# Soft-MoE behind a sliding-window attention: how two experts' w2 come in, as whole transfers or as 112 partitions and twice 8

## The chip, the cores and the metric

One core of one Trainium2 chip runs the whole program. The metric is the time of one execution on the device in microseconds, lower is better. "TensorE" is the matmul engine (PE), "VectorE" DVE, "ScalarE" ACT, "GpSimd" POOL, "SyncE" SP. Sixteen DMA engines move data between HBM and the core's on-chip memory of 128 partitions.

## The reference, cut to what matters

```python
# attention: q, k, v of [8, 8, 576, 64]; band of 32 for four heads, every fourth of 128 for the others
scores = np.where(mask, (q @ k.T) / 8, -1e9); attn = softmax(scores); x = (attn @ v) -> [4608, 512]

logits = x @ phi                                   # [4608, 32]: 8 experts of 4 slots
d = softmax over the 4608 rows of logits;  slot_input = d.T @ x
for e in range(8):
    slot_out[e] = np.maximum(slot_input[e] @ w1[e], 0) @ w2[e]   # w1 [512, 1024], w2 [1024, 512]
out = softmax over the 32 slots of logits @ slot_out             # [4608, 512], float32
```

All eight experts' output rows are needed before the first row of `out` can be made, so every w2 is needed first.

## The kernel before, in words

The order of the work is written out by hand (`manual_schedule`): each engine runs its instructions in the order of the program text. The eight batches go through attention in a pipeline (`ORDER`, `STEPS`). The inputs are float32 in HBM and are cast to half precision by the transfers on their way in, so all loads are issued by POOL, which is one queue, in order.

The loads, in POOL's order: for each batch two transfers each of raw Q, K and V (`load_raw`, L191, 64 partitions each); between them, from batch 3 on, one w1 of 1 MB (half precision) at a time (`load_w1`, L197); behind the last V the remaining w1 and the w2 of experts 0, 1 and 2 (`load_w2` without `s`, L205: one transfer of 128 partitions, 8 KB in each). Then a place in on-chip memory has to come free: the raw tiles and the slabs of Q and K are given back once the last transposes and scores of batch 7 have run (the test on `left`, L555). There w2 of experts 3 and 4 come as one whole transfer each (L205 again), and w2 of experts 5, 6 and 7 as twelve quarters of 256 KB (L211): the left 256 columns of 5, 6, 7 (two quarters each), then the right 256 columns.

Each load of POOL counts its landing on one of eight semaphores, in turn. An issue waits until the transfer eight issues before it, which used the same semaphore, has landed. So at most eight transfers are in flight, and where the queue is full POOL stands and waits for a landing before it issues the next.

After attention, PE multiplies the slots by all w1 (L616), transposes (L626), and sums w2 into two column halves `so0` and `so1` (`emit_so`, L646): experts 0 to 3 for both halves, expert 4 for both halves, then 5, 6, 7 for the left half, each as its quarters land. The left half is gathered and spread (L660, L665), and the first six batches of `out` are made for the left 256 columns (L672 on PE, L681 on ACT, L685 on DVE, sent by L692); the right half's experts 5, 6, 7 are worked in between, and `spread_so(1)` opens the rest of the output: six right halves, two whole batches, and the two transfers of left-over rows (L721). Output transfers are issued by POOL too, on the same queue behind the loads.

Of the kernel before, what the change touches and what calls it, by code (L numbers as in the profile page):

```python
# [10 lines left out]
FP16 = mybir.dt.float16  # L11
# [13 lines left out]
DMODEL = H * D  # L25
E_EXP = 8
S_PER_E = 4
N_SLOTS = 32
# [10 lines left out]
NP = 5  # L39
NFIN = N_ROWS // 128  # L40
DH = DMODEL // 2

GROUPS = (
    (("P", 0), ("P", 1), ("P", 2)),
# [3 lines left out]
ORDER = """  # L48
MD0.2 MK2.2 AP4.2 ET.3 VBc.1 S1.1 MK0.1 RP4.2 ED.3 E1.1 AD1.2 EP.3 VC.1 RD1.2 MP4.2
VCc.1 ER.3 MD1.2 AD3.2 VA.1 QT0.0 AP3.2 RD3.2 VAc.1 QT1.0 RP3.2 MD3.2 S2.1 KT1.0  # L50
# [45 lines left out]
def kernel(  # L96
# [10 lines left out]
    nc = tc.nc  # L107
# [5 lines left out]
    consts = ctx.enter_context(tc.tile_pool(name="consts", bufs=1))  # L113
# [9 lines left out]
    phi_raw = consts.tile([128, 4, N_SLOTS], FP16, name="phi_raw")  # L123
    phi4 = consts.tile([128, 4, 4, N_SLOTS], FP16, name="phi4")
    ones = consts.tile([128, 128], FP16, name="ones")
    ET = consts.tile([128, 192 * B], FP16, name="ET")
    UT = consts.tile([128, 5, N_SLOTS], FP32, name="UT")
    rcol = consts.tile([128, N_SLOTS], FP32, name="rcol")
# [9 lines left out]
    w2t = {e: w2a_pool.tile([128, 8, DMODEL], FP16, name=f"w2_{e}", tag=f"w2_{e}") for e in range(3)}  # L138
# [13 lines left out]
    def slab_weights(e, tag, n):  # L152
        t = fix.tile([128, n], FP16, name=f"w2_{e}", tag=tag)
        w2t[e] = t[:, 0 : 8 * DMODEL].rearrange("p (c n) -> p c n", c=8)
# [41 lines left out]
    def load_w1(e):  # L196
        nc.gpsimd.dma_start(  # L197
            out=w1t[e].rearrange("p (u c) f -> p u (c f)", u=2),
            in_=moe_w1[e].rearrange("(u p c) f -> p u (c f)", u=2, p=128),
        )  # L200

    def load_w2(e, s=None):
        src = moe_w2[e].rearrange("(p c) n -> p c n", p=128)
        if s is None:
            nc.gpsimd.dma_start(  # L205
                out=w2t[e].rearrange("p c n -> p (c n)"), in_=src.rearrange("p c n -> p (c n)")
            )
            return
        cols = slice(DH * s, DH * s + DH)
        for u in range(2):  # L210
            nc.gpsimd.dma_start(out=w2t[e][:, 4 * u : 4 * u + 4, cols], in_=src[:, 4 * u : 4 * u + 4, cols])  # L211
# [195 lines left out]
    def back_et(b, lp):  # L407
        nc.scalar.activation(out=ET[:, 192 * b : 192 * b + 192], in_=lp, func=AF.Exp, scale=1.0)

    def back_erow(b):  # L410
        m, l = et_cols(b)
        ep = ring.tile([128, 6, N_SLOTS], FP16, name=f"ep_{b}", tag="ring")
        left = ET[0:32, l : l + 128]
        nc.tensor.transpose(
            ep[:, 0:4, :].rearrange("p t s -> p (t s)"), ET[:, m : m + 128], ident
        )
# [14 lines left out]
    def back_erd(b):  # L431
        m = et_cols(b)[0]
        erd = s_pool.tile([128, DIL, N_SLOTS], FP16, name=f"erd_{b}", tag="erd")
        nc.vector.transpose(out=erd, in_=ET[:, m : m + 128].rearrange("p (a r) -> p r a", r=DIL))
        erd_t[b] = erd
# [38 lines left out]
    for which in "QK":  # L474
        load_raw(which, 1)
    nc.gpsimd.dma_start(
        out=phi_raw.rearrange("p (u c) s -> p u (c s)", u=2),
        in_=moe_phi.rearrange("(u p c) s -> p u (c s)", u=2, c=2),
# [4 lines left out]
    nc.vector.memset(ones, 1.0)  # L483
    nc.vector.memset(ET, 0.0)
    nc.vector.memset(siTm, 0.0)
# [10 lines left out]
    def step(op, b):  # L496
        if op[0] in "ARM" and op[1:] in TILES:
            kind, i = TILES[op[1:]]
            if op[0] == "A":
                tmp[(op[1:], b)] = emit_av(b, kind, i)  # L500
            elif op[0] == "R":
                tmp[("R" + op[1:], b)] = emit_recip(b, kind, i, tmp[(op[1:], b)])
            else:
                engine = nc.scalar if op[1:] in ON_ACT else nc.vector
                norm_mult(b, kind, i, tmp.pop((op[1:], b)), tmp.pop(("R" + op[1:], b)), engine)
        elif op in ("S0", "S1", "S2"):
            tmp[(op, b)] = emit_scores(b, int(op[1]))
        elif op in ("E0", "E1", "E2"):
            emit_exp(b, int(op[1]), tmp.pop(("S" + op[1], b)))
        elif op in ("MK0", "MK1", "MK2"):  # L510
            emit_mask(b, int(op[2]))
        elif op[0:2] in ("QT", "KT", "VT"):
            turn(op[0], b, int(op[2]))
        elif op in ("XP0", "XP1"):
            tmp[(op, b)] = xT_plain(b, int(op[2]))
        elif op in ("XD0", "XD1"):
            tmp[(op, b)] = xT_dil(b, int(op[2]))
        elif op in ("XPc0", "XPc1", "XDc0", "XDc1"):
            xT_copy(b, op[1], int(op[3]), tmp.pop((op[0:2] + op[3], b)))
        elif op in ("VA", "VB", "VC", "VD"):  # L520
            tmp[(op, b)] = v_rows(b, "ABCD".index(op[1]))
        elif op in ("VAc", "VBc", "VCc", "VDc"):
            v_place(b, "ABCD".index(op[1]), tmp.pop((op[0:2], b)))
        elif op in ("LG", "EP"):
            tmp[(op, b)] = (back_logits if op == "LG" else back_erow)(b)
        elif op == "ET":
            back_et(b, tmp.pop(("LG", b)))
        elif op == "ER":
            back_er(b, tmp.pop(("EP", b)))
        else:  # L530
            {"ED": back_erd, "U": back_u, "UT": back_add}[op](b)

    def loads(which, b):
        load_raw(which, b)
        if which == "V":
            if b > 2:
                load_weights(1)
            if b == B - 1:
                load_weights(len(weights))
# [5 lines left out]
    w2b_pool = None  # L545
    for it in range(B + max(s for _, s in STEPS)):
        for op, stage in STEPS:
            b = it - stage
            if not 0 <= b < B:
                continue  # L550
            step(op, b)
            if op in frees and b + 2 < B:
                loads(frees[op], b + 2)
            left.discard((op, b))
            if w2b_pool is None and not left:  # L555
                raw_pool.release()
                w2b_pool = tc.alloc_tile_pool(name="w2b", bufs=1, side="right")
                for e in (3, 4, 5):
                    w2t[e] = w2b_pool.tile([128, 8, DMODEL], FP16, name=f"w2_{e}", tag=f"w2_{e}")
                slab_weights(6, "qk0", QK_SLAB)  # L560
                slab_weights(7, "qk1", QK_SLAB)
                for e in (3, 4):
                    load_w2(e)
                for s in range(2):
                    for e in (5, 6, 7):
                        load_w2(e, s)
        if it == 0:
            nc.vector.tensor_copy(
                out=phi4, in_=phi_raw[:, :, None, :].broadcast_to([128, 4, 4, N_SLOTS])
            )  # L570
# [17 lines left out]
    for pr in range(B // 2):  # L588
# [11 lines left out]
        out=diag,  # L600
# [10 lines left out]
    for fc in range(2):  # L611
        for g in range(2):
            for dc in range(4):
                for j in range(4):
                    e = 4 * g + j
# [9 lines left out]
    for c in range(8):  # L625
# [3 lines left out]
        out=hTm[:, 0].rearrange("p c (j s) -> p c j s", j=4)[:, :, :, 0:16], in_=hT4[:, :, :, 0:16]  # L629
    )  # L630
    nc.scalar.copy(
        out=hTm[:, 1].rearrange("p c (j s) -> p c j s", j=4)[:, :, :, 16:32], in_=hT4[:, :, :, 16:32]
# [5 lines left out]
    om_l = h_pool.tile([128, B // 2, DMODEL], FP16, name="om_l", tag="om_l")  # L638
    so = [psum_so.tile([128, DH], FP32, name=f"so{s}", tag=f"so{s}") for s in range(2)]

    def emit_so(s, experts):
        for c in range(8):
            for e in experts:
# [4 lines left out]
                    hTm[:, g, c, 32 * j : 32 * j + 32],  # L648
                    w2t[e][:, c, DH * s : DH * s + DH],
                    start=(e < 4 and c == 0),  # L650
# [3 lines left out]
    def part_cols(s):  # L654
        c0 = DH * s
        return (nc.vector.tensor_copy, 0, c0), (nc.scalar.copy, DH // 2, c0 + DH // 2)

    def gather_so(s):
        for copy, c, c0 in part_cols(s):
            copy(out=so_part[:, c0 : c0 + DH // 2], in_=so[s][:, c : c + DH // 2])  # L660

# [58 lines left out]
    for e in range(2):  # L720
        nc.gpsimd.dma_start(  # L721
            out=rest[:, e, 512:576, :].rearrange("n i d -> i n d"), in_=om_l[64 * e : 64 * e + 64]
# [37 lines left out]
```

## Time and profile before

| what | value |
|---|---|
| median of 3 runs | 181.05 us (180.69 to 181.62) |
| the profiled execution | 180.9 us, its span 178.9 us |
| granted TensorE clock, mean | 0.853 |
| busy share of PE, DVE, ACT, POOL | 72%, 70%, 68%, 31% |
| chain that ended last: DMA, DVE, PE, ACT | 52%, 16%, 11%, 9% |
| of it, transfers of the weights | 36% |
| HBM read and written | 62.07 MB and 9.44 MB, 400 GB/s over the span |

The span is the profiled stretch; 2.0 us of the execution lie around it. The profile's DMA row gives, for 40 equal slices of 4.47 us, the mean busy share of the sixteen DMA engines in tenths, and the GB/s row what they moved, counted on the receiving side: a load receives half as many bytes as it reads from HBM, since it casts float32 to half precision, and an output transfer twice as many as it reads. A line of the DMA issues says how many transfers, how large on the receiving side, and how many microseconds from the issue to the last landing. A waiting time is put down to what ended it.

### The profile page before, as it was taken

The numbers are of one execution on the slowest core, as the hardware profiler recorded it, in microseconds if no ns is written. First come the engines' busy times: TensorE is split into PE (matmuls) and PEld (weight loads), VectorE is DVE, ScalarE is ACT, GpSimd is POOL, SyncE is SP. The second block draws the span as 40 slices with busy tenths as digits, with TensorE's granted clock in tenths as the row PEclk, the third lists the DMA queues.
The fourth block names the chain that finished last, engine by engine and source line by source line (L and its number), as shares of the span: only waits on it lengthen the run. The fifth ranks groups of instructions, "written<-read, shape, count | busy, mean of one in ns | idle before, by whom it ended". The sixth has DMA issues, their size and how long they took to land.

```text
span 178.9 us, 5405 instructions
## 1 busy us (share of the span) xinstructions
PE 128.0 (72%) x2316; PEld 84.7 (47%) x2316; DVE 125.7 (70%) x274; ACT 122.2 (68%) x267; POOL 56.2 (31%) x94
## 2 busy tenths in 40 slices
PE   0026838989999999989989999988695346688100
PEld 0014525676667767657767757856434112221000
DVE  6483999999999999999999995472402016789200
ACT  6007757999999999999999999966002016698100
POOL 7544244224224223243420041111112414376400
PEclk9999999999999879999999999687669955555555
DMA  5999999999999999999999999999999999999994
GB/s 91 203 213 208 214 212 210 214 212 216 214 212 213 215 212 215 214 212 216 210 214 215 212 218 220 215 216 220 211 212 191 197 196 219 390 319 397 406 413 135
DMA packets 21448, 40.88 MB, mean 229 GB/s; under 512 B 1713, under 2 KB 14129, under 8 KB 20785
## 3 DMA queue, kind: packets, MB, share of 16 engines
q0 software_dynamic: 21280, 40.41, 114.2%
q8 instruction: 18, 0.29, 0.6%
q1 hardware_dynamic: 144, 0.14, 0.3%
q14 instruction: 6, 0.04, 0.1%
HBM read 62.07 MB, written 9.44 MB: 400 GB/s over the span
## 4 chain that ended last, share of the span: by engine, by line
DMA 52%; DVE 16%; PE 11%; ACT 9%; issue 3%; POOL 2%; POOLq 0%; DVEq 0%
DMA w<-in_moe_w_dram 36%; DMA rawV<-in_v_dram 10%; DMA rawK<-in_k_dram 6%; DVE vT L222 5%; DVE qk L222 4%; DVE p L283 3%; PE f L672 3%; ACT p L272 3%; ACT om L681 2%; PE s L263 2%; PE o_P L313 2%; PE rv L237 2%; ACT xp L337 1%; PE rp L357 1%; ACT vX L243 1%
## 5 line engine op out<-in xcount | busy, mean ns | idle before, releaser
L272 ACT ACTIVATE p<-s 128x1728 f16<-128x1728 f32 (+1 forms) x24 | 42.0, 1749 | 10.7 <-PE s L263 10.6
L263 PE MATMUL s<-qk 32*128 32x144 f16 (+2 forms) x640 | 29.2, 325 | 16.1 <-DVE qk L222 12.3
L313 PEld LDWEIGHTS <-p 128*128 128x128 f16 (+3 forms) x672 | 23.9, 101 | 14.0 <-issue 3.6
L263 PEld LDWEIGHTS <-qk 32*128 32x128 f16 x640 | 17.0, 118 | 20.4 <-DVE qk L222 12.3
L337 ACT ACTIVATE xp<-o_P,rc_P 128x64 f16<-128x64 f32 x96 | 23.8, 384 | 2.4 <-DVE rc_P L325 2.3
L283 DVE TENSOR_TENSOR p<-p,masks 128x1728 f16<-128x1728 f16 (+1 forms) x24 | 25.4, 1082 | 0.0
L243 ACT COPY vX<-rv 128x512 f16<-128x512 f16 (+1 forms) x32 | 23.5, 786 | 1.7 <-PE rv L237 1.6
L313 PE MATMUL o_P<-vX,p 128*128 128x65 f16 (+1 forms) x288 | 20.7, 210 | 1.3 <-DVE xp L341 0.3
L222 DVE STREAM_TRANSPOSE qk<-rawQ 128x576 uint32<-128x576 uint32 x16 | 18.9, 1243 | 2.7 <-DMA rawQ<-in_q_dram 2.7
L222 DVE STREAM_TRANSPOSE qk<-rawK 128x576 uint32<-128x576 uint32 x16 | 19.7, 1241 | 0.5 <-DMA rawK<-in_k_dram 0.5
L222 DVE STREAM_TRANSPOSE vT<-rawV 128x576 uint32<-128x576 uint32 x16 | 19.6, 1238 | 0.4 <-DMA rawV<-in_v_dram 0.4
L237 PE MATMUL rv<-cst,vT 128*128 128x128 f16 x160 | 17.3, 248 | 3.0 <-DVE vT L222 1.7
L211 POOL DMA_DIRECT2D w<-in_moe_w_dram x12 | 8.9, 745 | 29.1 <-DMA w<-in_moe_w_dram 24.8
L685 DVE TENSOR_SCALAR om<-f,rrow 128x256 f16<-128x256 f32 (+1 forms) x28 | 13.5, 518 | 3.9 <-PE f L672 3.1
L237 PEld LDWEIGHTS <-vT 128*128 128x128 f16 x160 | 12.0, 127 | 8.6 <-issue 4.3
L191 POOL DMA_DIRECT2D rawQ<-in_q_dram x16 | 8.9, 557 | 21.5 <-DVE rc_P L325 16.3
L681 ACT ACTIVATE om<-f,rrow 128x256 f16<-128x256 f32 (+1 forms) x28 | 12.8, 503 | 3.3 <-PE f L672 2.6
L672 PE MATMUL f<-so_sb,ET 32*128 32x256 f16 (+1 forms) x60 | 12.1, 420 | 3.7 <-ACT om L681 2.4
L692 POOL DMA_DIRECT2D out_dram<-om x14 | 10.4, 747 | 12.1 <-DVE om L685 9.4
L191 POOL DMA_DIRECT2D rawK<-in_k_dram x16 | 8.7, 548 | 17.1 <-DVE rc_P L325 14.6
L191 POOL DMA_DIRECT2D rawV<-in_v_dram x16 | 8.7, 547 | 10.8 <-DVE rc_P L325 8.0
L372 ACT COPY xT<-rp 128x576 f16<-128x576 f16 x16 | 10.5, 776 | 1.2 <-PE rp L357 1.2
(84 smaller groups left out, 197.4 us busy)
## 6 DMA issues: line engine op xcount, KB each, us to landing
w<-in_moe_w_dram POOLq DMA_DIRECT2D x13, 1024.0 KB, 21.7
out_dram<-om POOLq DMA_DIRECT2D x12, 512.0 KB, 6.2
rawQ<-in_q_dram POOLq DMA_DIRECT2D x16, 288.0 KB, 10.7
rawK<-in_k_dram POOLq DMA_DIRECT2D x16, 288.0 KB, 10.4
rawV<-in_v_dram POOLq DMA_DIRECT2D x16, 288.0 KB, 10.2
w<-in_moe_w_dram POOLq DMA_DIRECT2D x12, 256.0 KB, 16.4
out_dram<-om POOLq DMA_DIRECT2D x2, 1024.0 KB, 8.6
out_dram<-om_l POOLq DMA_DIRECT2D x2, 512.0 KB, 9.1
```

The lines of the kernel that those rows point to most:

```text
L191: nc.gpsimd.dma_start(out=t[g::2, :], in_=src[4 * g : 4 * g + 4].rearrange("h (p j) d -> (h p) (j d)", j=PJ),)
L222: nc.vector.transpose(out=out_, in_=in_)
L237: nc.tensor.transpose(rg[:, n_t, :, c, :], rows, ident)
L243: copy(out=vX[b % 2][:, t0 : t0 + n, :, 0:D], in_=rg.rearrange("p n h c d -> p n h (c d)"))
L263: nc.tensor.matmul(sps[:, h, c0 : c0 + w], kk, qq, start=(tt == 0), stop=(tt == 1))
L272: return nc.scalar.activation(out=pt, in_=sps[:, :, 0:n], func=AF.Exp, scale=SCALE)
L283: return nc.vector.tensor_tensor(out=pt, in0=pt, in1=m, op=ALU.mult)
L313: nc.tensor.matmul(o[rows, h, :], lhs, rhs, start=(n == 0 or (kind == "L" and n < DIL)), stop=(n == len(jobs) - 1), skip_group_check=True,)
L337: nc.scalar.activation(out=dst[:, h], in_=src[:, h], func=AF.Copy, scale=rc[:, h : h + 1])
L672: nc.tensor.matmul(fp[:, 0 : c1 - c0], ET[32 * j : 32 * j + 32, m : m + 128], so_sb[32 * j : 32 * j + 32, c0:c1], start=True, stop=True,)
L681: nc.scalar.activation(out=dst, in_=fp[:, 0 : c1 - c0], func=AF.Copy, scale=rrow[:, blk : blk + 1])
L685: nc.vector.tensor_scalar(out=dst, in0=fp[:, 0 : c1 - c0], scalar1=rrow[:, blk : blk + 1], scalar2=None, op0=ALU.mult)
```

## The change

The two tiles of w2 of experts 3 and 4 become one tile `w2_34` of 128 partitions with the two experts side by side. Each expert's first 112 partitions come in one transfer. The last sixteen partitions, of both experts together, come in two transfers of 8 partitions, and in front of each a tiny one of 8 partitions copies 16 rows of phi (64 values in a partition) into a tile `aside` that nothing reads. The twelve quarters follow as before.

```diff
+EVEN = 112
+SKIP_FIRST = True
...
+    aside = consts.tile([8, 2, N_SLOTS + 16], FP16, name="aside")
...
+    def next_eight():
+        nc.gpsimd.dma_start(
+            out=aside[:, :, 0:N_SLOTS], in_=moe_phi[0:16].rearrange("(p u) s -> p u s", u=2)
+        )
+
+    def load_w2_pair(e, pair):
+        src = moe_w2[e : e + 2].rearrange("e (p c) n -> p e (c n)", p=128)
+        for i in range(2):
+            nc.gpsimd.dma_start(out=pair[0:EVEN, i], in_=src[0:EVEN, i])
+        for n, p in enumerate(range(EVEN, 128, 8)):
+            if n > 0 or SKIP_FIRST:
+                next_eight()
+            nc.gpsimd.dma_start(out=pair[p : p + 8], in_=src[p : p + 8])
...
-                for e in (3, 4, 5):
-                    w2t[e] = w2b_pool.tile([128, 8, DMODEL], FP16, name=f"w2_{e}", tag=f"w2_{e}")
+                pair = w2b_pool.tile([128, 2, 8 * DMODEL], FP16, name="w2_34", tag="w2_34")
+                for i in range(2):
+                    w2t[3 + i] = pair[:, i].rearrange("p (c n) -> p c n", c=8)
+                w2t[5] = w2b_pool.tile([128, 8, DMODEL], FP16, name="w2_5", tag="w2_5")
...
-                for e in (3, 4):
-                    load_w2(e)
+                load_w2_pair(3, pair)
```

POOL's order around the change, as the built programs have it, each with the semaphores waited for (SW0 to SW7 are the eight that count landings):

```
before                          after
w2_3  128 partitions  SW4       w2_34 first 112, expert 3   SW4
w2_4  128 partitions  SW5       w2_34 first 112, expert 4   SW5
w2_5  first quarter   SW6       aside, 8 partitions         SW6
...                             w2_34 112 to 119, both      SW7
                                aside, 8 partitions         SW6 and SW0
                                w2_34 120 to 127, both      SW1
                                w2_5  first quarter         SW2
                                ...
```

The second `aside` writes the tile that the first one writes; its wait for SW6 asks for one landing more than the first `aside` asked for, which is the first `aside`'s own. On PE, the first matmul on expert 3 waits for SW4, SW7 and SW1, where it waited for SW4 alone; the first on expert 4 waits for SW5 beside them.

## The prediction

> **What bounds the kernel now.** I read the page's slices first, then the chain that ended last, then POOL's issues in the timeline, then the time to landing of single transfers.
>
> ```profile
> DMA  5999999999999999999999999999999999999994
> GB/s 91 203 213 208 214 212 210 214 212 216 214 212 213 215 212 215 214 212 216 210 214 215 212 218 220 215 216 220 211 212 191 197 196 219 390 319 397 406 413 135
> ...
> q8 instruction: 18, 0.29, 0.6%
> ```
>
> The DMA engines are busy in every slice. Loads hold 210 to 220 GB/s (they read twice that) until about 153 us; from slice 35 the output runs at about 400. No compute engine is full over the span. So the time is set by when each DMA engine gets through its list, and any stretch in which the engine that ends last has nothing to do is lost. The last line above matters below: 18 code fetches of 16 KB ride on the same engines.
>
> In the chain of waits from 88 us on (start, length, what):
>
> ```profile
> 88.68 28.72 DMA w<-in_moe_w_dram
> 117.40 0.28 issue
> 117.68 25.39 DMA w<-in_moe_w_dram
> 143.08 0.28 issue
> 143.36 10.22 DMA w<-in_moe_w_dram
> 153.58 0.04 issue
> 153.62 0.43 PE so L646 x4
> ```
>
> One load lands, 0.28 us later POOL issues the next; the last quarter lands at 153.58, and only then the output's right half can start. POOL's timeline (start, length, then idle before and what ended it) around the change:
>
> ```profile
> 105.02 1.06 POOL L205 DMA_DIRECT2D w<-in_moe_w_dram  x2 [13.07 <-DVE rc_P L325]
> 106.06 0.77 POOL L211 DMA_DIRECT2D w<-in_moe_w_dram  x1
> 107.88 0.76 POOL L211 DMA_DIRECT2D w<-in_moe_w_dram  x1 [1.05 <-DMA w<-in_moe_w_dram]
> 113.08 0.74 POOL L211 DMA_DIRECT2D w<-in_moe_w_dram  x1 [4.45 <-DMA w<-in_moe_w_dram]
> 117.68 0.74 POOL L211 DMA_DIRECT2D w<-in_moe_w_dram  x1 [3.86 <-DMA w<-in_moe_w_dram]
> ```
>
> Experts 3 and 4 are issued at 105.02 and 105.54, the first quarter at 106.06; then POOL waits at each issue for the landing of the transfer eight before. The issues of DMA in the stretch from 106 to 106.5 us (kind, size, us to landing) show how deep the queue is:
>
> ```profile
> w<-in_moe_w_dram POOLq DMA_DIRECT2D x1, 1024.0 KB, 31.3
> w<-in_moe_w_dram POOLq DMA_DIRECT2D x1, 256.0 KB, 32.1
> ```
>
> Expert 4, issued at 105.54, lands 31.3 us later, at 136.87; the first quarter at 106.06 + 32.1 = 138.2. Transfers land in the order of issue, each when everything ahead of it has gone through. A landing is sixteen marks in the trace, one from each DMA engine; the first and last mark of the first quarter are 135.39 and 138.18, so the earliest engine runs 2.8 us ahead of the latest. At 24 us they were within 0.6. Eight engines are 2.2 to 2.8 behind, eight within 1.2; the packets show code fetches of 16 KB about every 6 to 13 us, and each puts one engine about 1.1 us back. I read it as: the fetches go round eight of the sixteen engines, which carry two each by then. Which eight these are by number the trace does not tell.
>
> **The change, part by part.**
>
> *The bytes.* The whole transfer of expert 2, issued at 91.42, lands 35.7 us later, at 127.10; then expert 3 at 132.02 and expert 4 at 136.87. So 1 MB takes 4.87 us, each engine's share of eight partitions 0.61 us a partition. The two transfers of 112 partitions are 7/8 of it: 2 x 4.26 = 8.5 us, so the last engine is through with them at 135.6 (the first at about 132.9). What is taken out, 2 x 0.61 = 1.2 us of an engine, returns in the transfers of 8. If such a transfer lies on eight engines, one partition each, and the tiny one has moved its place by eight, both large pieces fall on the same eight engines: these carry 18 rows of 8 KB instead of 16, the others 14. That is +1.2 us on one half, -1.2 on the other.
>
> *The wait that is added.* The second tiny transfer waits until the first has landed, because both write the same tile. The first is issued at about 106.1 (its semaphore came free at 102.7, 84.47 plus 18.2), behind both 112s; it lands when the engines come to it, at **135.7**. The pair's first piece is issued at 107.88, when the transfer eight before has landed, as the second quarter is now. Then POOL stands at the second tiny transfer for 28 us. Behind it on POOL's queue are the second piece of the pair and all twelve quarters. At 135.7 nothing is left for the engines but the first piece, 1.2 us on its eight engines. In the kernel before, seven quarters were in the queue at that time. This is the price, and it is a drained queue.
>
> *The restart.* From landing to issue 0.28 (the chain): the second tiny transfer at 136.0. It and the second piece cost POOL 0.54 to 0.74 each: nearest rows are the whole w2 transfers at L205 (538 ns) and the quarters at L211 (742 ns); phi's load, the nearest in shape, has 721. I take 0.6, with a gap of nothing: the first quarter is issued at about 137.2. From issue to landing with an empty queue there are two rows: the very first load (1.27 us, 4.2 us to landing, 288 KB), and the output transfer at 157.61 (4.3 us, 512 KB on its wide side, as a quarter's). In the latter, fourteen of sixteen engines have their mark by 3.4 us. So 3.4 to 4.3, plus up to 0.6 on the engines that have the second piece ahead: the first quarter lands between 137.0 + 3.4 = 140.4 and 137.4 + 4.3 + 0.6 = 142.3. I take 141.3, nearer to 3.4 because an empty queue has no late engines. Against 138.2 that is **+3.1 us** (2.2 to 4.1).
>
> *Behind it.* The other eleven quarters come every 1.33 us as now (landings 139.49, 140.90 and on), since POOL can issue one in 0.75 (outputs at 157.61 to 160 are that close). Nothing else binds: the semaphores of the tiny and small transfers are free by then. So the last quarter lands near 156.7, and the output's right half, opened by it, starts 3.1 later.
>
> *What hides other costs.* The matmuls on expert 3 now wait for the second piece, about 140, where the 88 of experts 0 to 4 and the first quarters ran at 137.03 for 2.79 us. They end near 143; the left half needs its sixth quarter, about 148, and each quarter's four matmuls take 0.3 to 0.4 us. That wait costs nothing; without the cover it would be about 3 us.
>
> *The end.* Does the tail give some back? Fourteen engines idle in the kernel before at about 158, waiting for the output issue at 157.61; they end in step, and the last transfer's marks lie within 0.35 us for these and at 0.97 and 1.26 us for the two that carried a fetch late. Those two never idle, so a delay before them goes through to the end. They will carry a fetch again after the restart, so I give nothing back. If they fell in step, it would be at most 0.9.
>
> The sum: 180.9 for the profiled execution + 3.1 = 184.0 us. That execution lies 0.15 below the median of 181.05; I keep 184.0.
>
> [...]
>
> **The rivals.**
>
> 1. *The balance is what counts* (ends faster). The eight late engines are the ones that lose two rows, and the tiny landing comes early enough to keep the queue filled. Late engines then gain 1.2 us: 179.7. For it: lateness really sits on eight engines. Against: it needs the second tiny transfer issued by about 133.2 (1.2 us for two issues and 1.4 until first data, the first load's 1.27 to its first packet at 2.63, before the late engines run dry at 135.6), and its predecessor is queued behind 8.5 us of rows that even the earliest engine finishes at 132.9. It decides from there.
>
> 2. *Only its own eight engines mark the tiny transfer, and they are the early ones.* It lands at about 134.0. The queue hardly runs dry for the late ones, which now carry 18 rows: +1.3, 182.2.
>
> 3. *The halves are mixed*, four late engines in each: the drain stays as it is, since the landing is that of the last engine. It is inside the forecast's bounds.
>
> 4. *The change does not put its rows on eight engines* (it does not do what it says): no half carries more, the drain alone remains, without the 0.6 for the second piece: +2.5, 183.4.
>
> **How the numbers follow.** Forecast (with the third rival) 0.74, at 184.0, from 183.1 to 185.0 by its bounds. The fourth rival 0.06. The second 0.07. The first 0.08. The remaining 0.05 I give to a case between the first two rivals, where the early landing and the shifted rows cancel and the time stays within 0.5% (0.9 us), about what a measurement of this kernel can tell from no change. Slower 0.74 + 0.06 + 0.07 = 0.87, same 0.05, faster 0.08. The range reaches down to the second rival and the 0.9 given back, 182.0, and up to the forecast's bound and the 0.15 of the median, 185.2.
>
> **What would show it.** In the timeline of POOL: the second tiny transfer with about 28 us of idle before it, ended by a DMA, at 135 to 137 us, and all twelve quarters behind it, 0.75 apart at first. In the slices: a dip of the DMA share and of GB/s in the slice at 134 to 143 us. In the marks: the first quarter's sixteen within about 1.2 us instead of 2.8. In the chain: a DMA on `aside`, and the last w landing at about 156.7. The forecast is wrong if POOL issues quarters before 133 us, if the dip is there but the last landing is not later than 154.5, or if the tail gives back more than 1 us.

## The result, and the profile after

| | before | after |
|---|---|---|
| median of 6 runs each, us | 180.9 (180.68 to 181.62) | 186.0 (185.32 to 186.84) |
| ratio, with its 95% interval | | 1.0263 (1.024 to 1.0286) |
| profiled execution, its span, us | 180.9, 178.9 | 185.63, 183.7 |
| granted clock, mean | 0.853 | 0.819 |

The change makes the kernel 5.1 us slower by the medians and 4.7 by the two profiled executions. The forecast said slower by 3.1 (184.0, range 182.0 to 185.2): the direction and the place are right, the size is not, and the time lies 0.8 above the range.

The page's slices (4.59 us each in this span) and its chain by engine, after:

```profile
DMA  5999999999999999999999999999938999999996
GB/s 105 188 210 211 213 210 211 215 213 214 212 213 216 209 219 211 214 211 215 210 218 212 214 219 218 219 212 218 207 70 83 189 192 196 341 383 398 402 414 178
...
q8 instruction: 18, 0.29, 0.6%
...
DMA 35%; DVE 30%; PE 15%; ACT 5%; POOL 4%; issue 4%; POOLq 0%; DVEq 0%
```

Before, every slice of the DMA row was a 9. Now the 30th and the 31st slice, 133 to 142 us, hold a 3 and an 8, and the loads fall from 207 to 70 and 83 GB/s. The code fetches are as many as before (18).

The chain of waits from 107 us on (start, length, what):

```profile
107.20 1.09 POOL w L213 x2
108.29 28.20 DMA aside<-in_moe_phi_dram
136.53 0.57 issue
137.10 0.55 POOL aside L206
137.65 0.56 POOL w L217
...
140.46 7.48 DMA w<-in_moe_w_dram
148.23 10.42 DMA w<-in_moe_w_dram
158.69 0.43 PE so L664 x4
```

A tiny transfer that nothing reads is now the longest piece of the path: issued at 108.29, landed at 136.5. The last quarter lands at 158.65 instead of 153.58. POOL's timeline (start, length, then the idle time before and what ended it):

```profile
107.20 1.09 POOL L213 DMA_DIRECT2D w<-in_moe_w_dram  x2 [14.53 <-DVE rc_P L342]
108.29 0.58 POOL L206 DMA_DIRECT2D aside<-in_moe_phi_dram  x1
108.87 0.58 POOL L217 DMA_DIRECT2D w<-in_moe_w_dram  x1
137.10 0.55 POOL L206 DMA_DIRECT2D aside<-in_moe_phi_dram  x1 [27.65 <-DMA aside<-in_moe_phi_dram]
137.65 0.56 POOL L217 DMA_DIRECT2D w<-in_moe_w_dram  x1
138.19 7.50 POOL L228 DMA_DIRECT2D w<-in_moe_w_dram  x10
```

In the kernel before, L211 issued seven quarters between 106 and 133 us. Now none of the twelve is issued before 138.19, and then ten go out back to back. The DMA issues between 137.5 and 139 us (kind, size, median us to landing) are what the restart costs:

```profile
w<-in_moe_w_dram POOLq DMA_DIRECT2D x2, 256.0 KB, 5.3
w<-in_moe_w_dram POOLq DMA_DIRECT2D x1, 128.0 KB, 4.8
```

The first two quarters take 5.3 us (5.12 and 5.55 one by one), where the forecast took 4.1.

### The profile page after: what moved, and what is told of

It is laid out like the page before. It is cut to its first block, busy times and chain, and to the rows that moved or that the text cites. A ratio compares the mean times of both kernels' runs of the same rounds, so it can differ in the third digit from the quotient of the medians.

```text
span 183.7 us, 5410 instructions
## 1 busy us (share of the span) xinstructions
PE 131.3 (71%) x2316; PEld 87.5 (48%) x2316; DVE 126.1 (69%) x274; ACT 122.8 (67%) x267; POOL 58.6 (32%) x98
## 4 chain that ended last, share of the span: by engine, by line
DMA 35%; DVE 30%; PE 15%; ACT 5%; POOL 4%; issue 4%; POOLq 0%; DVEq 0%
DMA aside<-in_moe_phi_dram 15%; DMA rawV<-in_v_dram 10%; DMA w<-in_moe_w_dram 10%; DVE vT L239 9%; DVE qk L239 8%; DVE p L300 6%; PE s L280 4%; PE rv L254 3%; PE f L690 3%; ACT om L699 2%; DVE xd L358 2%; PE o_P L330 2%; ACT p L289 2%; PE rp L374 1%; PE o_D L330 1%
## 5 line engine op out<-in xcount | busy, mean ns | idle before, releaser
L289 ACT ACTIVATE p<-s 128x1728 f16<-128x1728 f32 (+1 forms) x24 | 41.2, 1717 | 11.1 <-PE s L280 11.0
L330 PEld LDWEIGHTS <-p 128*128 128x128 f16 (+3 forms) x672 | 24.8, 103 | 14.4 <-issue 4.0
L280 PEld LDWEIGHTS <-qk 32*128 32x128 f16 x640 | 16.5, 118 | 21.0 <-DVE qk L239 12.7
L260 ACT COPY vX<-rv 128x512 f16<-128x512 f16 (+1 forms) x32 | 22.8, 750 | 2.2 <-PE rv L254 2.0
L330 PE MATMUL o_P<-vX,p 128*128 128x65 f16 (+1 forms) x288 | 21.2, 212 | 1.4 <-DVE xp L358 0.3
L254 PE MATMUL rv<-cst,vT 128*128 128x128 f16 x160 | 18.1, 257 | 3.3 <-DVE vT L239 1.8
L254 PEld LDWEIGHTS <-vT 128*128 128x128 f16 x160 | 12.5, 130 | 9.0 <-issue 4.3
L664 PE MATMUL so<-w,hTm 128*32 128x256 f16 x128 | 8.5, 398 | 7.1 <-DMA w<-in_moe_w_dram 6.6
L330 PE MATMUL o_D<-vX,p 128*128 128x65 f16 x128 | 10.4, 209 | 1.1 <-DVE xp L358 0.7
```

The source lines that it names most:

```text
L254: nc.tensor.transpose(rg[:, n_t, :, c, :], rows, ident)
L260: copy(out=vX[b % 2][:, t0 : t0 + n, :, 0:D], in_=rg.rearrange("p n h c d -> p n h (c d)"))
L280: nc.tensor.matmul(sps[:, h, c0 : c0 + w], kk, qq, start=(tt == 0), stop=(tt == 1))
L289: return nc.scalar.activation(out=pt, in_=sps[:, :, 0:n], func=AF.Exp, scale=SCALE)
L330: nc.tensor.matmul(o[rows, h, :], lhs, rhs, start=(n == 0 or (kind == "L" and n < DIL)), stop=(n == len(jobs) - 1), skip_group_check=True,)
```

## The experiments

Theory: the wait alone makes the loss, by emptying the queue. Rivals: the rows moved onto eight engines, the narrow pieces themselves, a slow start that belongs to the restart however much work lies ready. The ratios are to the kernel before on the same chip; its median was 181.25 us beside e1 to e4, 181.38 beside e5 to e8, 181.25 beside e9 to e12, and 181.16 beside e13 to e15. A ratio is taken over all runs and need not be that of the two medians to the last digit. The last column is of one profiled execution; that of e7 is the fastest of its seven runs (181.5).

| run | what it has | median us | ratio (95%) | last quarter landed, us |
|---|---|---|---|---|
| before | whole experts 3 and 4 | 180.9 | 1 | 153.58 |
| after | wait, tiny ones, narrow pieces | 186.0 | 1.0263 (1.024 to 1.0286) | 158.65 |
| e4_wait_only | the wait alone | 185.92 | 1.0256 (1.0237 to 1.0275) | 157.77 |
| e13_two_ahead | e4, two quarters ahead of the wait | 183.53 | 1.0129 (1.011 to 1.0147) | 155.65 |
| e14_four_ahead | e4, four quarters ahead | 181.33 | 1.0009 (0.9996 to 1.0023) | 153.61 |
| e15_wait_whole | e4, experts 5 to 7 whole | 193.32 | 1.0669 (1.0647 to 1.0691) | 156.12 |
| e1_two_tiles | after, without the wait | 183.28 | 1.0109 (1.0092 to 1.0127) | 155.96 |
| e2_behind | e1, each tiny one behind its piece | 182.19 | 1.0045 (1.0029 to 1.0061) | 155.15 |
| e3_no_tiny | narrow pieces alone | 182.15 | 1.005 (1.0037 to 1.0063) | 154.69 |
| e12_no_tiny_stride2 | e3, every second partition | 181.44 | 1.0008 (0.9999 to 1.0017) | 153.96 |
| e5_four_block | four narrow pieces of adjacent partitions | 182.57 | 1.0071 (1.005 to 1.0093) | 155.15 |
| e6_four_stride | the same, every fourth partition | 181.45 | 1.0006 (0.9993 to 1.0019) | 153.76 |
| e10_wait_stride2 | after, every second partition | 186.36 | 1.028 (1.0262 to 1.0299) | 159.17 |
| e11_behind_stride2 | e2, every second partition | 181.35 | 1.0008 (1.0 to 1.0017) | 154.34 |
| e9_small_first | e11, small ones ahead of the large | 181.2 | 1.0007 (0.9993 to 1.0021) | 154.11 |
| e7_stride_early | e6, tiny ones that load one half | 182.44 | 1.0052 (1.0032 to 1.0072) | 154.11 |
| e8_stride_late | e6, tiny ones that load the other half | 182.8 | 1.0084 (1.007 to 1.0099) | 155.56 |

### The wait alone

Against the kernel before, nothing else changed:

```diff
                 for e in (3, 4):
                     load_w2(e)
+                for _ in range(2):
+                    nc.gpsimd.dma_start(
+                        out=aside[:, :, 0:N_SLOTS], in_=moe_phi[0:16].rearrange("(p u) s -> p u s", u=2)
+                    )
```

> The kernel before, w2 of experts 3 and 4 as whole transfers of 128 partitions, with nothing added but the two tiny transfers into one tile behind them: the second waits for the first. No row changes its engine. Theory (wait and drain): POOL stands until about 137.5, the first quarter lands about 4 us later than before and the time is 184.5 to 186. Rival (18 rows on one half) and rival (narrow transfers are slow): 180.9 to 181.4, the price of two issues.

Measured 185.92, a ratio of 1.0256 against 1.0263 for the whole change. POOL's timeline of this kernel:

```profile
106.24 0.59 POOL L566 DMA_DIRECT2D aside<-in_moe_phi_dram  x1
137.21 0.56 POOL L566 DMA_DIRECT2D aside<-in_moe_phi_dram  x1 [30.38 <-DMA aside<-in_moe_phi_dram]
137.76 7.48 POOL L212 DMA_DIRECT2D w<-in_moe_w_dram  x10
```

No row of w2 has moved, and the loss is there in full. (The tiny transfers as such are not it: e14 below has the same two and costs 0.2 us.) The counterpart takes the wait away and leaves the rest:

```diff
-    aside = consts.tile([8, 2, N_SLOTS + 16], FP16, name="aside")
+    asides = [consts.tile([8, 2, N_SLOTS + 16], FP16, name=f"aside{i}") for i in range(2)]
```

with the first tiny transfer into `asides[0]` and the second into `asides[1]`.

> The changed kernel with a tile of its own for each of the two tiny transfers, so that the second waits for nothing but its semaphore's turn. Theory (the wait drains the queue, all of the +5 us is that wait and the restart): POOL issues the second tiny transfer at about 113 and the quarters from 123 to 145 us, no slice below 180 GB/s before the output, and the time is that of the kernel before plus or minus the 1.2 us of the rows that move between the halves: 182.1 if the half that gets 18 rows is the late one (the marks of the first narrow piece in the changed kernel point that way: seven of the eight late marks move by over a microsecond), 179.7 if it is the early one. Rival (the 18 rows on one half are the cost): nothing is won, 185 to 186 again. Rival (narrow transfers of 8 KB rows are slow in themselves, 3.3 us for two rows as in the changed kernel): 184 to 185.

Measured 183.28 (1.0109): not the 182.1 at most of the theory, nor the 184 to 185 of slow narrow pieces, but between. Its POOL never stands for long behind a tiny transfer:

```profile
113.06 0.55 POOL L206 DMA_DIRECT2D aside<-in_moe_phi_dram  x1 [3.37 <-DMA w<-in_moe_w_dram]
117.92 0.55 POOL L217 DMA_DIRECT2D w<-in_moe_w_dram  x1 [4.31 <-DMA w<-in_moe_w_dram]
122.72 0.80 POOL L228 DMA_DIRECT2D w<-in_moe_w_dram  x1 [4.25 <-DMA w<-in_moe_w_dram]
```

The first quarter goes out at 122.72 instead of 138.19, the lowest slice around it is 160 GB/s (70 in the change; the expectation had none below 180), and of the 5.1 us some 2.0 are left. The two runs do not add up (4.7 and 2.0 are more than 5.1). I read it as: while the queue is drained, the engines that carry more rows catch up with the others, which have nothing either; no run shows this alone.

### How much queued work covers the wait

In e13 the second tiny transfer stands behind the first two quarters, in e14 behind the first four, so that 2.7 or 5.3 us of work (1.33 a quarter) lie in the queue while POOL waits. In the place of e4's two tiny transfers and the loop of the quarters (`tiny()` issues one; each `load_w2` issues two quarters):

```diff
+                tiny()
+                for n, (s, e) in enumerate((s, e) for s in range(2) for e in (5, 6, 7)):
+                    if n == 1:                 # n == 2 in e14
+                        tiny()
+                    load_w2(e, s)
```

> As the run with the wait alone (two tiny transfers into one tile, no rows moved), but the second tiny transfer is issued after the first two quarters instead of in front of them, so that the waiting instruction has 2 x 1.33 = 2.7 us of queued work behind it. Theory (the wait costs the stretch in which the engines have nothing, some 5 us from the landing of the first tiny transfer to that of the quarter issued behind it, less the work that lies ready): last quarter 4.2 - 2.7 = 1.5 us later than before, some 155, total 182.5 to 183.5. Rival (the restart is slow however much lies ready, or the waiting instruction itself costs): last quarter at 157 or later, total 184.5 or more.

> The same with four quarters, 5.3 us of queued work, in front of the second tiny transfer. Theory: the work that lies ready covers the whole stretch of 5 us, the eight later quarters follow without a gap, total 181.0 to 181.8 and no dip of the slices under 150 GB/s. Rival: 182.5 or more, with the dip of GB/s moved some 5 us later but as deep.

Measured 183.53 and 181.33. The same wait now costs 2.4 us, and then 0.2, which cannot be told from nothing (the interval of its ratio reaches down to 0.9996). The first is 0.03 above the theory's bound and 1 us below the rival's; the second is inside, and its lowest slice is 165 GB/s, above the 150 that was named. POOL's timeline, e14:

```profile
108.59 0.59 POOL L566 DMA_DIRECT2D aside<-in_moe_phi_dram  x1
109.18 0.79 POOL L212 DMA_DIRECT2D w<-in_moe_w_dram  x1
...
122.39 0.74 POOL L212 DMA_DIRECT2D w<-in_moe_w_dram  x1 [3.83 <-DMA w<-in_moe_w_dram]
137.56 0.57 POOL L566 DMA_DIRECT2D aside<-in_moe_phi_dram  x1 [14.43 <-DMA aside<-in_moe_phi_dram]
138.13 5.97 POOL L212 DMA_DIRECT2D w<-in_moe_w_dram  x8
```

POOL still stands 14 us, and the quarters behind the wait go out at 138.1, as in e4. But the fourth quarter's last mark comes at 142.14 and the fifth's at 143.51: the latest engine never runs dry. So it is not the wait that costs, nor the standing POOL, but the time in which the engines that end last have nothing.

What a drained queue loses can be read as bytes. Windows of 3 us (the last two columns are the DMA share and GB/s), first the kernel before:

```profile
136.00:139.00 3.00, 2.48 (x80) 2.30 (x83) 0.42 (x1) 0.59 (x1) 1.27 (x2) 1.00 1.39 188
139.00:142.00 3.00, 1.10 (x28) 0.52 (x20) 0.00 (x0) 0.00 (x0) 1.69 (x3) 1.00 1.45 197
142.00:145.00 3.00, 0.79 (x8) 0.21 (x8) 0.00 (x0) 0.00 (x0) 0.74 (x1) 0.70 1.45 195
145.00:148.00 3.00, 1.34 (x10) 0.53 (x10) 0.72 (x3) 0.77 (x3) 0.00 (x0) 0.50 1.45 196
```

then e4, the wait alone:

```profile
136.00:139.00 3.00, 2.48 (x80) 2.30 (x83) 0.42 (x1) 0.59 (x1) 1.79 (x3) 1.00 0.05 6
139.00:142.00 3.00, 0.44 (x17) 0.25 (x9) 0.00 (x0) 0.00 (x0) 3.00 (x5) 1.00 1.04 132
142.00:145.00 3.00, 0.70 (x8) 0.21 (x8) 0.00 (x0) 0.00 (x0) 3.00 (x5) 0.59 1.26 147
145.00:148.00 3.00, 0.81 (x8) 0.23 (x8) 0.00 (x0) 0.00 (x0) 1.63 (x3) 0.50 1.41 181
```

and e14, with four quarters ready:

```profile
136.00:139.00 3.00, 2.07 (x24) 0.58 (x16) 0.19 (x1) 0.60 (x1) 1.44 (x3) 0.76 1.42 190
139.00:142.00 3.00, 1.93 (x32) 1.53 (x36) 0.93 (x2) 0.59 (x1) 3.00 (x5) 0.81 1.28 167
142.00:145.00 3.00, 3.00 (x80) 2.48 (x72) 0.00 (x0) 0.00 (x0) 2.10 (x3) 0.62 1.27 169
145.00:148.00 3.00, 1.63 (x29) 0.82 (x18) 1.43 (x5) 1.49 (x5) 0.00 (x0) 1.00 1.42 189
```

Against the kernel before, e4 lacks 310 GB/s summed over these four windows, and 63 in the one ahead of them (133 to 136 us: 134 against 197), where its early engines have already run dry. Times 3 us, divided by the steady 196, that is 5.7 us of the stream. It is not at full rate again until 148. By the same sum e13 lacks 3.3 and e14 0.9 us. Their costs are 4.7, 2.4 and 0.2, each 0.7 to 1.0 less: that part falls on the engines that were ahead. In e14 the last quarter's marks lie 1.7 us apart, where they lay 3.5 apart before, and the last of them is at the same place.

These windows also show what the forecast lacked: behind the restart the stream does not come at its full rate at once. The marks of e4's first quarters begin at 141.27, 142.64, 144.44, 146.08 and 147.42, so 1.4, 1.8, 1.6 and then 1.33 apart: 0.8 us lost after the first quarter was there. Taken place by place in the order of the sixteen marks, from this quarter to the fourth behind it, all of e4's marks lose 0.8 to 1.2 us. In e14 the same quarters' eight earliest marks lose 1.0 to 1.2 (they begin at 141.55, 142.98, 144.83, 146.52 and 147.85), and the other eight 0.1 to 0.2, the last 0.7. The eight early engines had run dry there (their next mark begins 2.1 us behind the fourth quarter's at 139.41, not 1.33), the others not: as far as the order of the marks tells, the slow start falls on engines that have run dry. One more run asked whether every restart is like this or only the quarters:

```diff
-                for s in range(2):
-                    for e in (5, 6, 7):
-                        load_w2(e, s)
+                for e in (5, 6, 7):
+                    load_w2(e)
```

> The run with the wait alone, but the w2 of experts 5, 6 and 7 come in whole transfers of 1 MB instead of two quarters for each half of the output, so the output starts later and only the restart is read. With the quarters the first ones behind the restart came 1.4, 1.8 and 1.6 us apart, and only the later ones 1.33. If the slow start belongs to the restart of any transfer, the first whole one lands 8.2 us or more after its issue (3.4 for an empty queue, 4.87 for its bytes, less the first quarter's part); if it belongs to the quarters (256 KB in rows of 512 or 1024 bytes, one issue each 0.75 us), the first whole one lands some 7.4 us after its issue and the next two 4.87 apart. Total several us over the kernel before, as the left half of the output has to wait for whole rows.

Measured 193.32; only the restart is read. The first whole transfer's marks lie from 7.33 to 8.58 us after its issue, the last one 0.6 behind the rest, and the next two follow 4.8 and 4.9 later. The two theories were put at 8.2 and 7.4, and the marks cover both, so the run does not decide. Its windows speak for the quarters: 145 GB/s from 139 to 142 us and 218 in the next, no third slow window. Why quarters behind a restart come in more slowly at first stays open. That POOL issues many in a row is not enough: in e14 the same issues feed the eight engines that lose and the eight that do not.

### The narrow pieces and the eight engines

Three runs take the balance apart without the wait. e2 moves each tiny transfer behind its piece, so that both pieces lie on the other eight engines; e3 has none, so the pieces lie on different halves and every engine carries 16 rows.

```diff
-            if n > 0 or SKIP_FIRST:
-                next_eight()                      # e2 and e3: gone from here
             nc.gpsimd.dma_start(out=pair[p : p + 8], in_=src[p : p + 8])
+            next_eight(n)                         # e2 only, two tiles
```

> As the run with two tiny tiles, but each tiny transfer stands behind its narrow piece, so that the two narrow pieces fall on the other half of the engines. Theory (wait and drain): again no drain, and the time lies on the other side of the kernel before than the run with the tiny ones in front, by the same 1.2 us: 179.7 if that one gives 182.1, with the last quarter's first and last mark at most 2.5 us apart instead of 3.5. Rival (18 rows on one half cost 5 us): if the first run is still at 185 to 186 this one falls to 181 or less. Rival (narrow transfers are slow in themselves): both stay at 184 to 186.

> The changed kernel without any tiny transfer: two of 112 partitions, two of 8, then the quarters. Theory (wait and drain): no wait, no drain, and each half gets one of the two narrow pieces, 16 rows on every engine: the time of the kernel before, 180.5 to 181.5. Rival (18 rows on one half): also 181, so it tells nothing between these two. Rival (narrow transfers are slow in themselves): 184 to 186.

The last quarter's sixteen marks tell where the rows went: in e1 they lie 4.7 us apart, in e2 2.2, in e3 3.1 (3.5 in the kernel before). So the tiny transfer does move the pieces by half the engines, one half or the other carries two rows more, and the predicted 1.2 us each way is there in size (4.7 and 2.2 lie 2.5 apart; e3, with equal rows, lies between). In time, e1 is 1.1 us slower than e3. Yet e2, which relieves the later half, is not faster: its first mark comes 2.8 us later than in the kernel before and its last 1.6 later, where the balance alone would give +1.2 and -1.2. And e3, which moves no load at all, costs 0.9 us. So e2 and e3 miss their theories (179.7; 180.5 to 181.5), and fall short of the 184 of their rival too. What they have in common is the pieces. Two runs cut the last 32 partitions into four pieces of 8, one in adjacent partitions, one in strides:

```diff
-        for p in range(EVEN, 128, 8):             # EVEN = 96, e5
-            nc.gpsimd.dma_start(out=pair[p : p + 8], in_=src[p : p + 8])
+        for p in range(EVEN, EVEN + 4):           # e6
+            nc.gpsimd.dma_start(out=pair[p:128:4], in_=src[p:128:4])
```

> No tiny transfers and no added wait; 96 partitions of each expert, then four narrow transfers of 8 adjacent partitions (96 to 103, 104 to 111, 112 to 119, 120 to 127) for both. Each half of the engines gets two of them, 16 rows on every engine. The run with two narrow ones and no tiny cost 0.9 us. Theory (eight engines that write into 8 adjacent partitions write slowly, because these share few ways into the memory): twice as many narrow pieces cost about twice as much, 182.5 to 183.5. [...] Rival (small pieces cost by their number, whatever their shape): also 182.5 to 183.5. Rival (the 0.9 us is the one joint tile, on whose last piece the matmuls wait): 182 as with two.

> As the run with four narrow transfers of adjacent partitions, but each takes every fourth of the 32 partitions (96, 100, .. 124; then 97, 101, ..). Same number of transfers, rows and engines. Theory (adjacent partitions share few ways into the memory): the eight engines write to eight places, the dip of the slices at 134 to 138 us goes, and the time is 181.0 to 181.8. [...] Rival (cost by number of pieces): as with adjacent ones, 182.5 to 183.5. Rival (joint tile): 182.

182.57 against 181.45: the same bytes, rows and number of transfers, and 1.1 us between them. The slices of GB/s around 134 us, e5 and then e6 (the 30th and 31st number, 168 149 and 206 185):

```profile
GB/s 99 205 210 208 215 210 212 214 212 215 214 211 215 213 211 215 213 212 214 212 212 218 214 216 218 221 209 227 207 168 149 196 197 217 388 319 399 404 414 129
```

```profile
GB/s 100 206 213 206 216 213 211 213 212 213 212 216 213 213 209 218 214 214 214 214 215 210 214 222 215 214 223 214 212 206 185 197 196 220 393 300 399 405 413 137
```

So the pieces of 8 adjacent partitions were slow in themselves. The trace has it in single rows too: those of 8 KB that move between 131 and 141 us take 0.81 us in the median in e5 and 0.62 in e6, as in the kernel before. The twin of e3 confirms it:

> Two of 112 partitions, two strided pieces, no tiny transfer, each half 16 rows. With adjacent partitions it was 182.15, 0.9 us over the kernel before. Theory (adjacent partitions): 181.0 to 181.6, the kernel before. Rival (number of transfers): 182.1 as with adjacent ones.

181.44 against e3's 182.15; and since e12 and e6 have the joint tile and lie within 0.2 us of the kernel before, the tile is not the cost. Adjacent partitions were thus the slower ones in both pairs of runs (by 1.1 and 0.7 us). Why, no run shows: the few ways into the memory of e5's and e6's theories are a guess of the author. Did this also make the restart slow? In the whole change with strided pieces,

> The changed kernel, its order and its wait as they are, but each narrow piece takes every second of the last sixteen partitions (112, 114, .. 126; then 113, .. 127). Theory (the wait drains the queue, and about a microsecond more than forecast is the narrow piece that writes into 8 adjacent partitions behind the restart): the wait of 27 us stays, the first quarter lands 4.3 to 4.6 us after its issue instead of 5.1, and the time falls by 0.4 to 1.0 us to 185.0 to 185.6, far from the kernel before. Rival (the whole 5 us is the narrow writing): falls to 182 or less. Rival (shape of the piece has no part in the restart): 186.0 as the changed kernel.

it measured 186.36, no gain. The second piece landed 3.8 us after its issue instead of 4.8, and the first quarter 4.80 after its own instead of 5.12, but the fourth quarter's marks began 8.47 us after the first quarter's issue, against 8.25 in the change as it is and 8.32 in e4, which has no piece in front. That guess fell: the narrow piece delays the first quarter, not the stream.

Can the move of rows gain anything without the wait and without adjacent partitions? Four runs: e11 (two pieces at a stride of two, a tiny transfer behind each), e9 (the same ahead of the two large transfers), e7 and e8 (four pieces at a stride of four, tiny ones placed so that three of four pieces lie on one half or on the other).

```diff
+        for n, p in enumerate(range(EVEN, EVEN + 4)):       # e7, EVEN = 96, two tiles
+            nc.gpsimd.dma_start(out=pair[p:128:4], in_=src[p:128:4])
+            if n > 1:                                       # e8: ahead of the piece, n in (0, 3)
+                next_eight(n - 2)
```

> A tile for each tiny transfer, each tiny one behind its narrow piece (early half carries 18 rows), pieces of every second partition. With adjacent partitions it was 182.2. Theory (that 0.9 us over the kernel before was what adjacent partitions cost, less what the moved rows gain): without the cost it gives 180.0 to 181.0. Rival (small transfers hold the eight semaphores, so the queue behind them is too shallow to gain): 181.3 to 182.2.

> As the run with each tiny one behind its strided piece, but the four small transfers stand ahead of the two of 112 partitions, so that they have landed long before the quarters are issued and the queue stays deep. Theory (lateness on one half sets the end, 0.6 us a row): 179.8 to 180.6, faster than the kernel before, whatever the run with the small ones behind gives. Rival (the end is not set by the half that is late during the loads): 181.0 to 181.8. If this one gains and the run with the small ones behind does not, the shallow queue is the difference.

> Strided narrow pieces, and two tiny transfers with a tile each behind the third and the fourth of them, so that the half of the engines that runs early carries three of the four pieces (18 rows) and the late half one (14 rows). Theory (each row of 8 KB moves an engine by 0.6 us, lateness on the late half sets the end): 1.2 us less than the run with four strided pieces and no tiny, 179.7 to 180.8, faster than the kernel before; first and last mark of the last quarter at most 2.3 us apart. Rival (the end is not set by the late half): as the strided run without tiny, 181 to 182.

> The mirror of the run with the early half loaded: tiny transfers ahead of the first and the fourth strided piece, so that the late half carries three of four pieces (18 rows). Theory (0.6 us a row on the late half): 1.2 us more than the strided run without tiny, 182.2 to 183, the marks of the last quarter about 4.5 us apart. Rival (the end is not set by the late half): as the strided run without tiny, 181 to 182.

None gains: 181.35, 181.2, 182.44 and 182.8 against 181.25 to 181.38. e11, e9 and e7 miss their theories, and e7 its rival too; e8's time was expected, but its marks lie 2.8 us apart and not 4.5. In e9 the last quarter's marks still spread over 4.2 us: two engines are 2 us ahead of all others, five stand 3.2 to 4.2 behind the first, and the last is at 154.11. With the late half relieved the spread should have shrunk to 2.3, as it did in e11. So some engines of the loaded half are late too, and one of them sets the end. The marks tell how many, though not which by number: in e1 the first narrow piece moves six of the eight late marks (135.49 to 136.08 become 137.03 to 137.57) and leaves two (135.21 and 135.26 become 135.42 and 135.48); in e8 it is six and two again. Whoever relieves the six loads the other two, and these then end last: in e11 the last quarter's last two marks, 154.27 and 154.34, stand 1.1 us behind all others. In e7 and e8 six small transfers hold six of POOL's eight semaphores, and the first quarters go out later (in e7 the first two at 130.97 and 134.94, in the kernel before at 106.06 and 107.88); e7's slices dip to 152 and 166 GB/s there, so its last quarter, though its marks lie within 1.3 us, comes at 154.11 (in its fastest run; the other six were 0.5 to 1.3 us slower).

## Why the prediction was wrong in size

By its own steps:

| step | forecast | measured | miss |
|---|---|---|---|
| what the second tiny transfer does | POOL stands some 28 us, the queue is drained | 27.65 us of idle, ended by `aside` | |
| first tiny transfer lands | 135.7 | 136.49 | +0.8 |
| from landing to issue | 0.28 | 0.57 | +0.3 |
| two issues ahead of the quarters | 1.2 | 1.09 | -0.1 |
| first quarter, issue to landing | 4.1 | 5.12 | +1.0 |
| eleven more quarters | 15.4 | 15.34 | -0.1 |
| last quarter lands | 156.7 (+3.1) | 158.65 (+5.1) | +2.0 |
| given back in the tail | 0, at most 0.9 | 0.33 | -0.3 |

The rows are of the profiled executions, which lie 4.7 us apart; 0.4 of the 5.1 between the medians is in no trace.

**The wait: right**, and shown. The second tiny transfer is issued 27.65 us late, by the landing of the first, and e4 and e1 put the loss on it. The place in the slices, the chain through `aside` and all twelve quarters behind it came as foreseen.

**The step that failed is the restart, mis-sized.** The prediction took 4.1 us from the first quarter's issue to its landing, by the first load and by an output transfer behind an idle stretch, and the full rate of 1.33 us a quarter from there on: 8.1 us to the landing of the fourth. Measured are 9.3 in e4, 9.8 in the change and 10.6 in e10. So the restart was put 1.2 to 2.5 us too short, and in the change 1.7.

In e4, where nothing stands in front, the row was nearly right for the first quarter (4.44), and the excess is the slow start behind it, 0.8 us by the earliest marks, which the prediction put at nothing. In the change it lies ahead of the first quarter's landing: with the adjacent piece in front that comes 5.12 us after its issue, with a strided one (e10) 4.80, and behind it the marks begin 1.35 apart from the second quarter on. By the fourth quarter the earliest marks are equally late in all three (8.32, 8.25 and 8.47 us after the first quarter's issue, where 3.4 and three times 1.33 make 7.4), so the narrow piece, costed at up to 0.6, is not what made the restart too long. The rest is that the engines, in step at the first quarter (0.5 us apart in the change), are 1.5 apart again from the third on. Why the start is slow stays open.

The rows that 4.1 came from could not show it. Behind the first load of all, the next ones have their earliest mark every 1.4 us (4.95, 6.34, 7.73; 288 KB each), and behind the output at 157.61 every 1.3, both the steady rate at once. And the output's row was no empty queue: fourteen engines marked the transfer ahead of it between 157.63 and 159.58, after its issue.

The step "every 1.33 us as now" reads as right, 15.34 for 15.4, but only because the 15.40 of the kernel before held a late engine's 0.8 us in its fourth quarter (landings 140.90 and 143.08); after, 2.07 us stand between the second and the third. That the two agree is luck.

**The landing of the tiny transfer** was worked out from expert 2's landing at 127.10. In the profiled execution after, that was already 128.00, with one engine 0.6 us behind the next; so +0.8 is the scatter of late engines between executions as much as an error of the step (e10, with the same large transfers: 136.20). Within it, the two large pieces took 8.0 us instead of 8.5, and the tiny one 0.5 behind them instead of 0.1. The 0.57 from landing to issue against 0.28 stays open; e4 has 0.28, e14 0.56.

**The range** had its upper end from the restart's two rows. Each of the small terms above (landing, issue, piece in front, slow start) was taken at its middle or at nothing, and they fell on the same side.

One reading was off without bearing on the sum: the marks lay within 0.6 us until 22.5, and 1.3 apart at 24.6.

**What hides other costs: right.** PE waits for the second piece and then runs its 88 matmuls late:

```profile
142.53 5.07 PE L664 MATMUL so<-w,hTm 128*32 128x256 f16 x89 [3.19 <-DMA w<-in_moe_w_dram]
147.99 0.29 PE L664 MATMUL so<-w,hTm 128*32 128x256 f16 x4 [0.40 <-DMA w<-in_moe_w_dram]
```

They took 5.07 us instead of 2.79 and ended at 147.6, not near 143, yet the next four still wait 0.40 us for the landing of a quarter, and the left half needs the sixth quarter, which lands at 150.62. So nothing of it reaches the end. That they run at a granted clock of 0.50 (142 to 145 us), where in the kernel before they ran at 1.00 (136 to 142), is hidden in the same way.

**The rivals.** The first (balance gains) fell for the reason it gave: the second tiny transfer was issued at 137.10, not by 133.2. Without the wait it gained nothing either (e11 and e9). The second (only its own eight engines mark the tiny transfer) fell: the first tiny transfer's sixteen marks spread from 133.16 to 136.49, like those of the large one ahead of it. The third (halves mixed) is partly true: six late engines in one half and two in the other, not four and four (e1, e8). The fourth (rows not on eight engines) fell: of the second piece's sixteen marks, eight lie at 139.10 to 139.17 and eight at 142.41 to 142.49.

The forecast's 135.7 takes it that a transfer of 8 partitions lands only when the last of all sixteen engines has reached it, the +1.2 and the 0.6 that its rows lie on eight. No run showed either ahead of the result; the trace of the change shows both: sixteen marks for each such transfer (the first tiny one's last at 136.49, the large one's ahead of it at 136.01), and the second piece's sixteen rows of 8 KB moving eight at a time, from 139.47 to 140.91.

## What to carry to other kernels

What a transfer cost here that waited for an earlier one of the same queue was the time in which the engines ran dry: 4.7 us with nothing queued between the two (e4), 2.4 with 2.7 us of transfers (e13) and 0.2 with 5.3 (e14). So give a dummy or double transfer its own tile (e11: 181.35), or put enough other transfers between the two, and look in the slices for a hole before looking at anything else. When a restart is sized from a single transfer's time to landing, add what stands in front of it, and what the first transfers lose below full rate (0.8 to 1.2 us in e4).

## What the runs showed of the hardware

- A queue of 256 KB transfers that had run empty was not at full rate when its first one had landed: in e4 (earliest mark 141.27) 147 GB/s from 142 to 145 us, against 195 in the kernel before. With transfers of 1 MB (e15) it was 218 in the same window. In e14 each of the quarters behind the restart lost 1.0 to 1.2 us at its eight earliest marks, by their order those of the engines that had run dry, and 0.1 to 0.2 at the others, 0.7 at the last.
- Eight adjacent partitions were slower to fill than eight at a stride: 182.57 against 181.45 us for four such pieces of 128 KB, 182.15 against 181.44 for two.
- The late DMA engines were not one of the two halves of the sixteen on which pieces of 8 partitions lie: in e1 and e8 six of the eight were in one and two in the other. With two rows moved from the same half to the other, the last quarter's marks spread over 2.3 us in e11 and over 4.2 in e9, and neither ended sooner than the kernel before (154.34 and 154.11 against 153.58).
